# Softmax attention and windowed attention, gated together: other landing times for SyncE's transfers in the planner, and another table of thresholds

## The chip, the cores and the metric

The kernel runs on one core of one Trainium2 chip. The metric is the device time of one execution in microseconds (us). Three executions of the kernel before took 815.80, 822.54 and 823.12 us; their median is 822.54 us. One further execution was profiled; it took 826.73 us, and the span from its first to its last instruction is 824.9 us.

Short names: PE is TensorE (matmuls; PEld its weight loads), DVE is VectorE, ACT is ScalarE, POOL is GpSimd, SP is SyncE, which issues nearly all DMA transfers.

## What is computed

Two attentions over the same x (2048 tokens, 640 features, 32 heads of 20), mixed by a gate. A is full softmax attention, B a causal one over 8 positions that lie 2 apart.

```python
x = A_x
g = _sigmoid((x * gate_w).sum(-1, keepdims=True))
a = _A_ref(x, A_wqkv, A_wo)      # softmax(q k^T / sqrt(20)) v, all 2048 keys, then @ wo
b = _B_ref(x, B_wqkv, B_wo)      # keys at s, s-2, ..., s-14 only, then @ wo
return g * a + (1 - g) * b
```

## The kernel before, in words

**Work on attention A.** The 2048 queries are cut in four chunks of 512, the heads in eight groups of four; that makes 32 groups (`GROUPS`), worked one after the other. A group has 16 key blocks x 4 heads = 64 units. For one unit PE multiplies a 128-key block with 512 queries (L1553) into a PSUM bank, the exponential is taken, and PE multiplies the result with v into the bank `obank` (L1617). The exponential of most units is ACT's (L1576, two or three units in one instruction, called a tile). The four units of a key block may instead go to DVE, as a "quad": DVE turns the scores into int16 numbers that are read as bf16 powers of two (L1566, "ride"), then adds a constant three times (L812), and PE multiplies all four versions with weighted copies of v (`vS`, made by POOL at L805). So a unit on DVE relieves ACT and costs DVE and PE more. At a group's end `gen_norm` (L773) transposes, divides and gates the result, and SP moves it into `oTd` with 4 or 5 transfers (L792).

**The queries.** `gen_qd` (L660) projects 128 features of q at a time: SP loads the weights `WqP` (`wq_load`, L634), PE multiplies, DVE scales into `dst`, SP spreads the rows over the padded `qT` buffers with 3, 7 or 8 transfers (L681), and a bound on the score goes in with 4, 8 or 12 small ones (L721).

**Work on attention B.** Eight units u of 256 tokens. For each, `gen_bproj` projects q, k, v; `gen_b` (L873) multiplies q with shifted k on DVE (L883), sums on PE, takes maximum and exponential, and sends a reciprocal to all partitions by SP in two steps (`rB`, L965 with 4 transfers and L967 with 3). `gen_v4` (L1013) has SP write shifted copies of v into `stage` with 16 transfers (L1017); DVE multiplies them by the probabilities (L981), PE sums, DVE writes `oB` (L1006). `gen_fold` and, at the end, `gen_prefold`, `gen_prefold2` and `tail` multiply `oTd` and `oB` with the output weights.

**The order of the work** is fixed when the kernel is built, by a planner in the kernel's own source. `_Sched.task` (L194) keeps a planned time for each engine: an instruction starts when its engine is free and what it depends on has ended, and ends after a duration that the caller names. For a DMA step the caller names the time from issue to landing; SP is held for `iss * nd`, 0.75 us for each of the `nd` transfers, whatever the landing time:

```python
        if dma:
            self.avail[stream] = start + iss * nd
            t.end = start + dur
```

Side work (everything but scores, exponentials and v products) consists of generators that yield requests such as `("dve", ahead, ready)`; `step` (L1170) grants one only when the planned clock says that its input is ready and its engine is not too far ahead. `ready` and `free` (L167, L175) read the planned ends. So a landing time is a promise on which the order of PE's, DVE's and ACT's instructions is built. On the chip every engine then works off its list in that order and waits on semaphores: if a transfer lands later than promised, the engine whose list has the reader next stands still, with everything behind it in its list.

`PLAN` (L50) sets 21 thresholds anew at tile numbers 0, 10, 20, ... (in the main loop from L1724): how much a tile may be followed by side work (`SLACK`), how late a third bank may come free (`XTOL`), when a quad may be opened for DVE (`DWAIT`, `DIDLE`, `DIDLE2`, `DTIME`, read in `wanted`, L1429), below which PE load filler matmuls are put in (`FILL`, read in `filler`, L1624), and so on. The kernel before has 721 tiles and 90 quads (360 rides at L1566).

Of the kernel before, what the change touches and what calls it, by code (L numbers as in the profile page):

```python
# [334 lines left out]
def _build(ctx, nc, A_x, A_wqkv, A_wo, B_wqkv, B_wo, gate_w, out):  # L335
# [4 lines left out]
    T = sch.task  # L340
# [18 lines left out]
    WqP = sb([P, CN, P], BF16, "WqP")  # L359
# [24 lines left out]
    TQ = TOK // 4  # L384
    tB = sb([P, TQ], FP32, "tB")
    rQ = sb([P, TQ], FP32, "rQ")
# [20 lines left out]
    rB = sb([P, TOK], FP32, "rB")  # L407
# [252 lines left out]
    def gen_qd():  # L660
        while not done.get(("q", 1)):
            yield ("cond",)
        n = 0
# [1148 lines left out]
```

## Time and profile before

| What | Value |
|---|---|
| three executions | 815.80, 822.54, 823.12 us |
| profiled execution | 826.73 us, span 824.9 us |
| ACT busy | 786.5 us (95%), of it L1576 775.1 us in 721 instructions |
| PE busy | 762.3 us (92%) |
| DVE busy | 708.6 us (86%) |
| POOL busy | 146.8 us (18%) |
| mean granted TensorE clock | 0.993 |
| first exponential starts, last one ends | 19.6 us, 812.2 us |

The profile is read from the engine that is busy nearly all the time towards what makes it stand still. "Idle" of an engine is listed with what ended it: `A <- B: total, times, longest`. The planner's own times are not in the profile; the profile has only what the chip did. The trace also has the time at which each transfer's semaphore was raised; a landing time below is the time from the start of the first issue of a step to the last of these.

### The profile page before, as it was taken

How to read it: one execution, taken by the hardware profiler on the slowest of the kernel's cores; microseconds unless marked ns; L12 is line 12 of the kernel's file. 1: busy time of each engine (PE TensorE's matmuls, PEld its weight loads, DVE VectorE, ACT ScalarE, POOL GpSimd, SP SyncE). 2: the span in 40 equal slices, each digit the busy share in tenths (PEclk: the TensorE clock that was granted, in tenths of full speed). 3: DMA queues.
4: the chain of work that ended last, by engine and by line, in shares of the span. 5: the costliest groups of instructions: out<-in, count | busy, mean ns of one | idle time of the engine just before them, and what ended most of it. 6: DMA issues, size and time to landing. Idle time of an engine off the chain costs nothing.

```text
span 824.9 us, 28923 instructions
## 1 busy us (share of the span) xinstructions
PE 762.3 (92%) x12201; PEld 277.6 (34%) x12201; DVE 708.6 (86%) x1255; ACT 786.5 (95%) x753; POOL 146.8 (18%) x203
## 2 busy tenths in 40 slices
PE   8999999999899999999999999899898999888888
PEld 5332223334333333333333334333332343322223
DVE  7578877698899999989988998899799989998963
ACT  4999999999999999999999999999999999999984
POOL 5040032330112111112111201111011111201110
PEclk9999999999999999999999999999999999999999
DMA  9112222001210311013003111300310030102001
GB/s 312 35 27 52 46 46 72 18 14 34 64 36 21 78 23 36 22 23 76 20 20 71 33 31 22 78 18 7 74 23 21 23 78 18 33 21 63 6 6 35
DMA packets 61397, 35.72 MB, mean 43 GB/s; under 512 B 27204, under 2 KB 60068, under 8 KB 61268
## 3 DMA queue, kind: packets, MB, share of 16 engines
q1 hardware_dynamic: 60980, 33.54, 16.5%
q8 instruction: 97, 1.59, 0.8%
q10 hardware_dynamic: 288, 0.33, 0.1%
q14 instruction: 32, 0.26, 0.1%
HBM read 11.94 MB, written 2.62 MB: 18 GB/s over the span
## 4 chain that ended last, share of the span: by engine, by line
ACT 34%; PE 28%; issue 16%; DVE 15%; SPq 4%; DMA 2%; POOL 0%; ACTq 0%; DVEq 0%
ACT ebuf L1576 33%; PE score L1553 8%; PE side L574 7%; PE obank L1617 7%; SPq L1017 4%; DVE uD L812 4%; DVE uD L1566 3%; DVE stage L883 3%; PE score L574 2%; DVE stage L981 1%; DMA stage<-qkvB 1%; DVE qkvB L867 1%; DMA oTd<-oN 1%; PE score L1265 1%; PE obank L475 1%
## 5 line engine op out<-in xcount | busy, mean ns | idle before, releaser
L1576 ACT ACTIVATE ebuf<-score 128x1024 bf16<-128x1024 f32 (+2 forms) x721 | 775.1, 1241 | 17.4 <-PE score L1553 16.7
L1553 PE MATMUL score<-qT,kT 32*128 32x512 bf16 x2048 | 288.0, 386 | 42.2 <-ACT ebuf L1576 28.6
L1566 DVE TENSOR_SCALAR uD<-score 128x512 int16<-128x512 f32 x360 | 240.7, 680 | 27.7 <-PE score L1553 26.2
L812 DVE TENSOR_SCALAR uD<-uD 128x2048 int16<-128x2048 int16 x270 | 185.7, 708 | 15.5 <-PE obank L1617 14.2
L1617 PE MATMUL obank<-ebuf,vA 128*21 128x512 bf16 x1688 | 167.6, 388 | 2.8 <-POOL vS L805 1.2
L1553 PEld LDWEIGHTS score<-qT,kT 32*128 32x128 bf16 x2048 | 70.6, 91 | 285.4 <-ACT ebuf L1576 211.7
L805 POOL TENSOR_TENSOR vS<-vA,vw 128x252 bf16<-128x252 bf16 x90 | 69.4, 777 | 301.4 <-PE obank L1617 277.8
L574 PE MATMUL side<-xT,kvw 128*32 128x256 bf16 (+2 forms) x2320 | 97.9, 286 | 4.2 <-DVE qkvB L867 2.8
L1617 PE MATMUL obank<-uD,vS 128*21 128x512 bf16 x1080 | 96.7, 385 | 0.1
L1617 PEld LDWEIGHTS obank<-ebuf,vA 128*21 128x21 bf16 x1688 | 41.4, 88 | 102.4 <-issue 75.1
L574 PEld LDWEIGHTS side<-xT,kvw 128*32 128x32 bf16 (+1 forms) x2320 | 55.3, 96 | 37.6 <-issue 15.0
L781 POOL TENSOR_TENSOR rcp<-rcp,gA 128x16 f32<-128x16 f32 x31 | 7.6, 247 | 310.9 <-DVE rcp L779 310.9
L981 DVE TENSOR_TENSOR stage<-stage,eB 128x1280 bf16<-128x1280 bf16 x64 | 53.0, 856 | 6.8 <-DMA stage<-qkvB 6.8
L883 DVE TENSOR_TENSOR stage<-qkvB 128x1280 bf16<-128x1280 bf16 x64 | 52.0, 841 | 0.2
L867 DVE CAST qkvB<-side 128x512 bf16<-128x512 f32 (+1 forms) x62 | 36.0, 590 | 3.2 <-PE side L574 3.1
L787 POOL TENSOR_TENSOR oN<-oTt,rcp 128x512 bf16<-128x512 f32 x31 | 32.6, 1052 | 2.4
L574 PE MATMUL side<-woBp,oB 128*32 128x512 bf16 (+1 forms) x540 | 29.1, 317 | 3.6 <-DMA oTd<-oN 1.6
L1617 PE MATMUL obank<-uD,vA 128*21 128x512 bf16 x360 | 32.3, 385 | 0.0
L574 PE MATMUL side<-woA_d,oTd 128*32 128x512 bf16 (+1 forms) x540 | 29.8, 309 | 0.0
L1617 PEld LDWEIGHTS obank<-uD,vS 128*21 128x21 bf16 x1080 | 26.0, 91 | 9.6 <-issue 3.0
L775 DVE STREAM_TRANSPOSE oTt<-obank 128x512 f32<-128x512 f32 x32 | 22.6, 706 | 3.4 <-PE obank L1617 3.3
L1638 PE MATMUL side<-xT,ident 128*32 128x512 bf16 x324 | 24.2, 381 | 0.0
(182 smaller groups left out, 535.7 us busy)
## 6 DMA issues: line engine op xcount, KB each, us to landing
stage<-qkvB SPq DMA_DIRECT2D x128, 82.5 KB
WqP<-in_A_wqkv_dram SPq DMA_DIRECT2D x16, 160.0 KB
stage<-in_B_wqkv_dram SPq DMA_DIRECT2D x1, 2400.0 KB
oTd<-oN SPq DMA_DIRECT2D x108, 20.0 KB
qT<-dst SPq DMA_DIRECT2D x104, 20.0 KB
out_dram<-outsb SPq DMA_DIRECT2D x12, 160.0 KB
kvw<-in_A_wqkv_dram SPq DMA_DIRECT2D x2, 800.0 KB
oTd<-in_A_x_dram SPq DMA_DIRECT2D x2, 640.0 KB
```

What stands on the lines that cost most here:

```text
L574: ins = e.matmul(o[j:k, :], l(j) if callable(l) else l[:, j:k], r, start=(first and i == 0), stop=(last and i == n - 1), skip_group_check= ...
L787: T(en, c2, lambda e: e.tensor_tensor(oo, ii, ib, ALU.mult), reads=["rcp", "oTt"], writes=["oN0"])
L805: T("pool", 0.7, lambda e: e.tensor_tensor(vS[:, d % NVS, :, :], _ap(vA, (kb * NQ + q) * 4 * DV, [[0, K - 1], [1, 4 * DV]]), _ap(vw, 0, [[ ...
L812: T("dve", 0.066 + 0.1334 * n, lambda e, k=k: e.tensor_scalar(uD[u][:, 0:512 * n].bitcast(I16), uD[u][:, 0:512 * n].bitcast(I16), SHIFTS[k ...
L867: t = TB(dvc(n * TOK), lambda e, o=o, i=i: e.tensor_copy(o, i), reads=[("side", b)], writes=[key])
L883: TB(dvc(CN * TOK, 2), lambda e, w=w, ks=ks: e.tensor_tensor(prodB(w), qB[:, :, :], ks, ALU.mult), reads=["qB", "kB"], writes=[("prod", w) ...
L981: TB(dvc(CN * TOK, 2), lambda e, o=o, vs=vs, ee=ee: e.tensor_tensor(o, vs, ee, ALU.mult), reads=["eB", ("prod", k)], writes=[("prod", k + ...
L1017: T("sp", 12.0, lambda e: [e.dma_start(bass.AP(tensor=stage, offset=32 * w4 * 4 * CN * (VW + TOK) + c * VW, ap=[[4 * CN * (VW + TOK), 32], ...
L1553: ins = e.matmul(o, kT[32 * j:32 * j + 32, q, kb * P:(kb + 1) * P], qT[g % NQT][32 * j:32 * j + 32, :], start=True, stop=True)
L1566: t = T("dve", 0.6, lambda e: e.tensor_scalar(uD[d % NU][:, 512 * i:512 * (i + 1)].bitcast(I16), side[x], UOFF, 0.0, op0=ALU.add, op1=ALU. ...
L1576: exps[s] = T("act", actc(512 * n), lambda e: e.activation(ebuf[s % NE][:, 0:512 * n], score[s % 2][:, 0:512 * n], ACTF.Exp, scale=LN2 / S ...
L1617: ins = e.matmul(obank[32 * j:32 * j + DV, :], v, src, start=(kb == 0), stop=(last and k >= len(lst) - 4), skip_group_check=True)
```

## The change

Seven charges, all of DMA steps on SP, get other landing times; `iss`, the number of transfers and all dependencies stay. And all rows of `PLAN` are replaced (64 before, 67 after); the code that reads it is the same.

| step | transfers | charge before (us) | charge after (us) |
|---|---|---|---|
| L637 weights to `WqP` | 1, 2 | 3.0, 3.5 | 4.5, 5.0 |
| L681 rows to `qT` | 3, 7, 8 | 3.5, 5.5, 6.0 | 4.24, 7.36, 8.14 |
| L721 bounds to `qT` | 4, 8, 12 | 4.0, 6.0, 8.0 | 4.5, 7.1, 9.7 |
| L792 results to `oTd` | 4, 5 | 4.0, 4.5 | 5.02, 5.8 |
| L965 reciprocals | 4 | 4.0 | 4.7 |
| L967 reciprocals | 3 | 3.5 | 4.2 |
| L1017 shifted v | 16 | 12.0 | 13.8 |

```diff
-        T("sp", 2.5 + 0.5 * len(parts), lambda e: [e.dma_start(WqP[:, :, a:a + n], wA_v[:, :, d:d + n]) for a, d, n in parts],
+        T("sp", 4.0 + 0.5 * len(parts), lambda e: [e.dma_start(WqP[:, :, a:a + n], wA_v[:, :, d:d + n]) for a, d, n in parts],
...
-                T("sp", 2.0 + 0.5 * len(pc), lambda e, i=i, pc=pc, qc=qc: [e.dma_start(
+                T("sp", 1.9 + 0.78 * len(pc), lambda e, i=i, pc=pc, qc=qc: [e.dma_start(
...
-                T("sp", 2.0 + 0.5 * 4 * len(runs), lambda e, runs=runs, qc=qc: [e.dma_start(
+                T("sp", 1.9 + 0.65 * 4 * len(runs), lambda e, runs=runs, qc=qc: [e.dma_start(
...
-            T("sp", 2.0 + 0.5 * len(pc), lambda e: [e.dma_start(
+            T("sp", 1.9 + 0.78 * len(pc), lambda e: [e.dma_start(
...
-        T("sp", 2.0 + 0.5 * 4, lambda e: [e.dma_start(rB[0:32, j * TQ:(j + 1) * TQ], rQ[32 * j:32 * j + 32, :]) for j in range(4)],
+        T("sp", 4.7, lambda e: [e.dma_start(rB[0:32, j * TQ:(j + 1) * TQ], rQ[32 * j:32 * j + 32, :]) for j in range(4)],
...
-        spread = lambda: T("sp", 2.0 + 0.5 * 3, lambda e: [e.dma_start(rB[32 * i:32 * i + 32, :], rB[0:32, :]) for i in range(1, 4)],
+        spread = lambda: T("sp", 4.2, lambda e: [e.dma_start(rB[32 * i:32 * i + 32, :], rB[0:32, :]) for i in range(1, 4)],
...
-        T("sp", 12.0, lambda e: [e.dma_start(
+        T("sp", 13.8, lambda e: [e.dma_start(
```

The rows of `PLAN` have the columns SLACK (two numbers), XTOL, XPRIO, XLATE, DWAIT, DIDLE, DIDLE2, DTIME, DLOW, DLATE, DVE_AHEAD, DAHEAD, BOOST, XBOOST, RFILL, FILL, HOLD, BOFF, BNEED, PVMIN, MAXQ. Three of the rows, before and after:

```diff
-    0: ((0.3, 0.64), 0.32, 2.5, 2.5, 0.49, -1.3, -0.1, 11.8, 7.0, 7.2, 0.52, 0.47, 4.4, 4.0, 0.0, 0.75, 2, -3, 0.38, 4.0, 3.0),
+    0: ((0.3, 0.64), 0.37, 2.5, 2.5, 0.49, -1.3, -0.1, 11.87, 7.0, 7.2, 0.52, 0.47, 4.4, 4.0, 0.0, 0.75, 2, 0.0, 0.45, 4.0, 4.0),
...
-    450: ((0.35, 0.67), 0.21, 6.6, 2.5, 0.78, -1.31, 0.45, 12.98, 6.7, 7.79, 0.67, 0.71, 4.6, 5.77, 0.08, 0.69, 2, 0, 0.55, 4.0, 3.0),
+    450: ((0.32, 0.67), 0.69, 2.5, 2.5, 0.8, -1.3, 0.24, 12.65, 6.7, 8.73, 0.57, 0.52, 4.4, 4.5, 0.01, 0.67, 1, -3, 0.45, 4.0, 2.0),
...
-    650: ((0.35, 0.67), 0.21, 2.5, 2.5, 0.78, -1.31, 0.45, 12.98, 4.5, 7.79, 0.77, 0.71, 5.28, 5.56, 0.08, 0.69, 1, 0, 0.46, 4.0, 3.0),
+    650: ((0.36, 0.66), 0.6, 2.5, 6.6, 0.49, -1.52, -0.25, 12.98, 7.0, 6.67, 0.52, 0.53, 4.4, 4.0, -0.04, 0.78, 2, 1, 0.49, 4.0, 3.0),
```

Over the 721 tiles, each row weighted by the tiles for which it holds, the mean of `DIDLE2` goes from 0.14 to -0.03, of `DIDLE` from -1.35 to -1.47, of `XTOL` from 0.30 to 0.56, of `FILL` from 0.69 to 0.77.

125 rows, old and new, of the table PLAN are left out of this document.

## The prediction

> **What bounds the kernel now.** I read the busy times first, then what ended ACT's idle time, then the timelines around its largest gaps, then the granted clock there.
>
> ```profile
> PE 762.3 (92%) x12201; PEld 277.6 (34%) x12201; DVE 708.6 (86%) x1255; ACT 786.5 (95%) x753; POOL 146.8 (18%) x203
> ```
>
> ACT is the bound: its exponentials run from 19.6 to 812.2 us, and only 17.4 us in between are idle. Time comes from there: from ACT's idle time, or from units that go to DVE. The waits of ACT, DVE and PE (us in total, times, longest) say who ends idle time:
>
> ```profile
> ACT ebuf L1576 <- PE score L1553: 16.7, 16, 2.4
> DVE stage L981 <- DMA stage<-qkvB: 6.8, 4, 2.1
> PE side L574 <- DMA oTd<-oN: 1.6, 1, 1.6
> ```
>
> ACT waits for scores alone, so the question is what made the scores late. The second and third line are candidates: DVE stood four times for the shifted copies of v, PE once for a group's result. Two timelines show one of them from both sides. DVE, then ACT:
>
> ```profile
> 529.67 0.69 DVE L812 TENSOR_SCALAR uD<-uD 128x2048 int16<-128x2048 int16 x1
> 532.46 0.82 DVE L981 TENSOR_TENSOR stage<-stage,eB 128x1280 bf16<-128x1280 bf16 x1 [2.10 <-DMA stage<-qkvB]
> ```
>
> ```profile
> 531.82 2.81 ACT L1576 ACTIVATE ebuf<-score 128x1536 bf16<-128x1536 f32 x2
> 536.31 1.02 ACT L1576 ACTIVATE ebuf<-score 128x1024 bf16<-128x1024 f32 x1 [1.68 <-PE score L1553]
> 538.24 1.02 ACT L1576 ACTIVATE ebuf<-score 128x1024 bf16<-128x1024 f32 x1 [0.91 <-PE score L1553]
> 539.75 2.37 ACT L1576 ACTIVATE ebuf<-score 128x1536 bf16<-128x1536 f32 x2 [0.48 <-PE score L1553]
> ```
>
> DVE's list has L981 next and stands for 2.10 us; the evictions of qkvB behind it come late, PE waits 2.12 us for one (a projection is next in its list, then scores), and 1.4 us after DVE went on ACT runs dry, three times in a row. The same picture stands at three other places. ACT near the end of the span:
>
> ```profile
> 794.87 4.13 ACT L1576 ACTIVATE ebuf<-score 128x1536 bf16<-128x1536 f32 x3
> 801.40 1.45 ACT L1576 ACTIVATE ebuf<-score 128x1536 bf16<-128x1536 f32 x1 [2.39 <-PE score L1553]
> 803.46 1.45 ACT L1576 ACTIVATE ebuf<-score 128x1536 bf16<-128x1536 f32 x1 [0.61 <-PE score L1553]
> ```
>
> and PE there, with the fold ahead of the scores in its list:
>
> ```profile
> 798.94 1.87 PE L574 MATMUL side<-woBp,oB 128*32 128x512 bf16 x16 [1.63 <-DMA oTd<-oN]
> 800.74 0.61 PE L1553 MATMUL score<-qT,kT 32*128 32x512 bf16 x3
> ```
>
> The busy times by stretch (PE, PEld, DVE, ACT, POOL, then the granted clock) show what follows such a stop:
>
> ```profile
> 532.80:536.20 3.40, 1.54 (x46) 1.09 (x46) 3.40 (x7) 1.83 (x2) 0.59 (x1) 1.00 0.03 9
> 536.20:539.60 3.40, 3.40 (x32) 0.70 (x29) 2.83 (x6) 2.05 (x2) 1.11 (x1) 0.50 0.00 0
> ```
>
> After a stretch in which PE was busy for 1.54 of 3.40 us, the clock is 0.50 for the next 3.4 us; this is why ACT runs dry again at 538 and 540. The clock's records have just three such windows between the start and the tail, at 536.2, 597.6 and 799.0 us, each behind a landing wait.
>
> **ACT's idle time by cause.** Behind the wait at 216.5 us: 1.42. Behind 532.5: 1.68 + 0.91 + 0.48 = 3.07. Behind 594.3: 1.98 + 0.69 + 0.91 = 3.58. Behind 798.9: 2.39 + 0.61 = 3.00. Sum 11.07 of 17.4 us. The rest is 2.05 at 21 us, before any of these steps, and bits of at most 0.5.
>
> **The change part by part.** It removes and adds no instruction of its own; it moves them. Its charges against the landing times in the trace (shortest, median, longest):
>
> - L1017, 12.0 to 13.8: traced 12.6, 13.6, 15.2. The longest three (14.2, 14.7, 15.2) are those behind which ACT ran dry; a fourth wait of 0.9 us cost ACT nothing.
> - L792, 4.5 to 5.8 for five transfers: traced 4.7, 5.0, 6.7; the 6.7 is the one before the fold.
> - L681 with seven, 5.5 to 7.36: traced 6.4, 6.8, 7.9. L721 with twelve, 8.0 to 9.7: traced 8.4, 9.0, 9.4; with eight, 6.0 to 7.1: traced 5.3, 5.4, 6.1.
> - L965, 4.0 to 4.7: traced 3.6, 4.2, 5.0. L967, 3.5 to 4.2: traced 3.0, 3.1, 4.3. L637, 3.0 to 4.5: traced 2.4, 2.5, 4.5.
>
> So the old charges were short of the trace where an engine stood (L1017, L792, L681), and the new ones are above the median everywhere, for L637 by 2.0 us.
>
> *Term 1, the waits for shifted v.* They were 1.83, 2.10, 1.98 and 0.9 us. With readers placed 1.8 us later, 0.03, 0.30, 0.18 and 0 are left. *Term 2, the fold.* PE stood 2.1 us from the end of its matmuls (their records leave 1.63); L792 gets 1.3 more, so 0.8 is left. Together 1.3 us of waits remain, and I charge ACT with the same 1.3. The clock windows should go with the waits: 11.07 - 1.3 = 9.8 us saved. Bounds: nothing, if landings slip as much again; all 11.1, if none does. What is late next at these places is the scores behind L981's neighbours, which are ACT's normal feed.
>
> *Term 3, what the larger charges push back.* The q chain (L637, L681, L721) is planned up to 1.5 + 1.86 + 1.1 = 4.5 us later for each group. It is hidden: q of a group landed 25 us or more before the group ahead of it closed, in all groups from the fourth on, and 12.7 us in the one before. In group 2 it was 4.6 us (landed at 72.2, group 1 closed at 76.8); scores start some 2.7 us (three tiles) before a close, so with that cover gone 4.5 - (4.6 - 2.7) = 2.6 us once. I take 0, since scores waited for qT only 0.2 us in the whole span. The B chain gets 1.8 + 0.7 + 0.7 = 3.2 us for each of 8 units, 25.6 if none of it is hidden; the last L1006 starts at 769.6 and the fold at 798.9, so 29 us hide it. If it were not hidden, POOL's copies and SP's later steps behind L1017 would be late too; I take 0. SP's own list is charged 0.75 us for a transfer as before, and is idle 129 us before L637 alone.
>
> *Term 4, the table.* No row shows where it leads, since it changes every decision. Its currency is the quad. An exponential of two units takes 0.90 us from start to start, one of three 1.33, so a unit is 0.44 to 0.45 us and a quad 1.8 us of ACT; on DVE it is four rides and three shifts at about 0.6 us from start to start, 4.2 us. Gain at most: DVE is idle 56 us between 170 and 790 us, 13 quads, 23 us, though that idle time is in bits of 1 us. Loss at most: from 100 us on, stretches of 50 us held 4.0 to 7.7 quads with a mean of about 6; the leanest throughout would be 2 fewer in each of 14, 28 quads, 50 us. The columns lean to the gain: DIDLE2 falls from a mean of 0.14 to -0.03, so quads open while DVE is less idle, and FILL rises, which keeps PE busier. But a threshold is no count; I take 0, nearest to the row that stays, 90 quads.
>
> **Sum.** 826.7 - 9.8 = 816.9 on the profiled execution. The median of the three shown, 822.54, is 4.2 us lower than it. If the unprofiled executions have all of these stops, the time is 822.5 - 9.8 = 812.7; if the profiled one merely had more of them (the fastest, 815.8, is 10.9 below it, about the size of the 11.07), it is 816.9. I take the middle, 815.
>
> A rule to weigh: the Trainium skill ("TensorE: Matmul & The Clock Gate", Part 1) has the clock halve after at least one idle window of about 3.4 us. PE's stops here were 2.1 to 2.2 us and the clock fell all the same, so the trace does not bear out a whole idle window as the condition.
>
> **Rivals.**
>
> 1. *The low clock is not the stops' doing*, and three such windows stay wherever they fall. For it: one stop (216.5 us, PE waits as DVE stood 1.83) had no window behind it. Against: all three windows stand behind stops. Then only ACT's first gaps go, 1.42 + 1.68 + 1.98 + 2.39 = 7.5, less 1.3: 6.2 us saved, 815 + 3.6 = 818.6. The skill's rule, taken by its word, would lead here.
> 2. *The waits move.* Landings of L1017 spread over 2.6 us, and a new order puts other transfers beside them (14.2 to 15.2 where L792, L965 or L967 followed closely). If they slip again by what they slipped, nothing is gained: 822.
> 3. *The table gives DVE more*: four quads more, 815 - 7.2 = 808. For it DIDLE2 and DVE's 6.8 us of waits that come free (1.6 quads); against it PE at 92%.
> 4. *Slower: the table gives DVE less*, because the planner now sees DVE's inputs and banks come later and refuses quads in `wanted`. Price 1.8 us for each quad. It undoes the 7.5 us gained against the median at four quads lost, and is slower by 1% (above 830.8) from nine lost, so 81 or fewer; 833 at ten. For it: the leanest stretches above. Against: DIDLE2.
>
> **How the numbers follow.** Chances: likeliest (815, give or take 5) 0.45; rival 1 0.10; rival 2 0.12; rival 3 0.15; rival 4 0.18. A difference of 1% is about what a measurement of this kernel can tell from none: 814.3 to 830.8 counts as the same. A little under half of the likeliest lies below 814.3 (0.22), with rival 3 that makes 0.37 faster; the other 0.23 with rivals 1 and 2 makes 0.45 the same; 0.18 slower. Range: 805, which leaves out rival 3 with six or more quads (0.05), to 830, which leaves out most of rival 4 (0.14).
>
> **What the profile of the changed kernel would show.** Terms 1 and 2: DVE's wait at L981 for stage under 1.5 us in total, PE's for oTd under 1, ACT's idle time before L1576 about 8 us in place of 17.4, no or one window of clock 0.50 between 20 and 810 us. Term 3: scores waiting for qT still under 1 us, and the last L1006 before 797. Term 4: rides at L1566, now 360; each four are 1.8 us. Wrong it would be if the count of rides is under 324, or if ACT is idle as long as before behind other waits.

## The result, and the profile after

The kernel after takes 814.56 us (median of 11 executions, 813.62 to 815.09), the kernel before 820.05 us in the same comparison (11 executions, 815.80 to 823.59): ratio 0.9941, 95% interval 0.9918 to 0.9965, so 5.5 us or 0.6% less. The profiled executions differ by more: 826.73 us before, 815.09 us after, spans 824.9 and 813.3 us. The executions of the kernel after also lie within 1.5 us, those of before within 7.8 us.

The busy times of the kernel after, and its waits (us in total, times, longest):

```profile
PE 772.4 (95%) x12439; PEld 279.5 (34%) x12441; DVE 704.3 (87%) x1248; ACT 787.4 (97%) x758; POOL 138.9 (17%) x202
```

```profile
ACT ebuf L1579 <- PE score L1556: 5.7, 7, 2.1
```

ACT's waits for scores fall from 16.7 to 5.7 us, and 4.1 of these are the two at the start that were there before (2.09 us ahead of the first exponential, 2.05 us ahead of the one at 23 us). (Line numbers are three higher in the kernel after: L984 was L981, L1020 was L1017.) No line of DVE's waits names a landing of `stage` any more and none of PE's a landing of `oTd`. DVE where the largest landing stood nearest to its reader, then PE at the last fold:

```profile
219.01 0.69 DVE L815 TENSOR_SCALAR uD<-uD 128x2048 int16<-128x2048 int16 x1
219.79 1.56 DVE L984 TENSOR_TENSOR stage<-stage,eB 128x1280 bf16<-128x1280 bf16 x2
221.27 0.68 DVE L1569 TENSOR_SCALAR uD<-score 128x512 int16<-128x512 f32 x1
```

```profile
788.47 0.61 PE L1620 MATMUL obank<-uD,vS 128*21 128x512 bf16 x8
788.90 0.61 PE L577 MATMUL side<-woBp,oB 128*32 128x512 bf16 x8
789.44 0.39 PE L1556 MATMUL score<-qT,kT 32*128 32x512 bf16 x3
```

At 219.79 L984 begins 0.02 us after its landing, with DVE busy until 219.70: the new order has no slack at this place. At 788.9 the fold begins 6.2 us after SP issued L795 (782.69), with scores right behind it instead of a stop of 1.63 us (by the matmul records). The clock's records have no window at half speed between the start and the tail.

Where the 11.6 us between the two spans are (before, then after: busy, mean ns, idle before):

```profile
L1576 ACT ACTIVATE ebuf<-score 128x1024 bf16<-128x1024 f32 (+2 forms) x721 | 775.1, 1241 | 17.4 <-PE score L1553 16.7
L1579 ACT ACTIVATE ebuf<-score 128x1024 bf16<-128x1024 f32 (+1 forms) x726 | 776.0, 1235 | 6.6 <-PE score L1556 5.7
```

ACT's idle time before its exponentials went from 17.4 to 6.6 (10.8 less); the end after the last exponential from 12.7 to 11.1 (1.6 less); the exponentials themselves from 775.1 to 776.0 busy (0.9 more), as there are 356 rides instead of 360. The remaining 0.1 is rounding and the start.

### The profile page after: what moved, and what is told of

It reads as the page before. It is cut to its first block, busy times and chain, and to the rows that moved or that the text cites. A ratio compares the mean times of both kernels' runs of the same rounds, so it can differ in the third digit from the quotient of the medians.

```text
span 813.3 us, 29378 instructions
## 1 busy us (share of the span) xinstructions
PE 772.4 (95%) x12439; PEld 279.5 (34%) x12441; DVE 704.3 (87%) x1248; ACT 787.4 (97%) x758; POOL 138.9 (17%) x202
## 4 chain that ended last, share of the span: by engine, by line
ACT 41%; PE 29%; issue 17%; DVE 12%; SPq 1%; DMA 0%; ACTq 0%; DVEq 0%
ACT ebuf L1579 40%; PE score L1556 9%; PE obank L1620 7%; PE side L577 5%; DVE uD L815 3%; DVE uD L1569 3%; PE score L577 2%; DVE stage L984 1%; SPq L1020 1%; DVE stage L886 1%; DVE qkvB L870 1%; PE side L1641 1%; PE score L1268 1%; PE obank L478 1%; PE obank L1641 1%
## 5 line engine op out<-in xcount | busy, mean ns | idle before, releaser
L1579 ACT ACTIVATE ebuf<-score 128x1024 bf16<-128x1024 f32 (+1 forms) x726 | 776.0, 1235 | 6.6 <-PE score L1556 5.7
L1569 DVE TENSOR_SCALAR uD<-score 128x512 int16<-128x512 f32 x356 | 238.3, 681 | 29.7 <-PE score L1556 28.2
L808 POOL TENSOR_TENSOR vS<-vA,vw 128x252 bf16<-128x252 bf16 x89 | 62.3, 710 | 280.0 <-PE obank L1620 247.0
L577 PE MATMUL side<-xT,kvw 128*32 128x256 bf16 (+1 forms) x2300 | 95.7, 283 | 1.6 <-DVE qkvB L870 1.0
L577 PEld LDWEIGHTS side<-xT,kvw 128*32 128x32 bf16 x2300 | 55.2, 96 | 32.8 <-issue 14.6
L984 DVE TENSOR_TENSOR stage<-stage,eB 128x1280 bf16<-128x1280 bf16 x64 | 52.2, 843 | 0.1
L1641 PE MATMUL side<-xT,ident 128*32 128x512 bf16 x404 | 30.0, 382 | 0.0
L577 PE MATMUL side<-woA_d,oTd 128*32 128x128 bf16 (+3 forms) x540 | 29.0, 298 | 0.0
L1641 PE MATMUL obank<-xT,zero 128*32 128x512 bf16 x328 | 26.8, 381 | 0.0
```

The lines of the kernel that those rows point to most:

```text
L577: ins = e.matmul(o[j:k, :], l(j) if callable(l) else l[:, j:k], r, start=(first and i == 0), stop=(last and i == n - 1), skip_group_check= ...
L808: T("pool", 0.7, lambda e: e.tensor_tensor(vS[:, d % NVS, :, :], _ap(vA, (kb * NQ + q) * 4 * DV, [[0, K - 1], [1, 4 * DV]]), _ap(vw, 0, [[ ...
L984: TB(dvc(CN * TOK, 2), lambda e, o=o, vs=vs, ee=ee: e.tensor_tensor(o, vs, ee, ALU.mult), reads=["eB", ("prod", k)], writes=[("prod", k + ...
L1569: t = T("dve", 0.6, lambda e: e.tensor_scalar(uD[d % NU][:, 512 * i:512 * (i + 1)].bitcast(I16), side[x], UOFF, 0.0, op0=ALU.add, op1=ALU. ...
L1579: exps[s] = T("act", actc(512 * n), lambda e: e.activation(ebuf[s % NE][:, 0:512 * n], score[s % 2][:, 0:512 * n], ACTF.Exp, scale=LN2 / S ...
L1641: ins = e.matmul(o[32 * j:32 * j + 32, :], w[:, 32 * j:32 * j + 32] if best else w[:, :], xT[:, 0, 0:512], start=bool(best), stop=bool(bes ...
```

## The experiments

Two theories. W: the new charges place readers where the transfer has landed, so that no engine stops, and that is the gain. T: the new table makes a better order by itself (more fillers, wider tiles). The first four runs, and the two with one and with six transfers more, keep an order of PE, DVE, ACT and POOL exactly as it is and move only the landing on the chip; this is done with fewer or more transfers in one step of SP, whose charge for issuing is kept in sum. So they change the wait and nothing that is planned. On the chip SP's later steps move a little with it, since SP issues its transfers one after the other (16 of them at L1017 took 11.0 to 12.7 us in the kernel before). The times below come from three comparisons in which the kernel before took 820.05, 819.11 and 819.28 us, so a difference of up to 0.9 us between two comparisons tells nothing.

### The order of before, shifted v landing earlier

```diff
-  ... for w4 in range(4) for c in range(4)],
-  reads=["vB"], writes=[("prod", w) for w in range(WIN)], dma=True, nd=16)
+  ... for w4 in range(4) for c in range(4) if w4 < 3 or c < 1],
+  reads=["vB"], writes=[("prod", w) for w in range(WIN)], dma=True, nd=13, iss=12.0 / 13)
```

> The kernel before with the instructions of PE, DVE, ACT and POOL in the same order, one for one; of the 16 transfers at L1017 three are left out (three shifted copies of v are missing from the output), SP's charge for issuing stays 12.0 us in all. So L1017 lands some 3 x 0.72 = 2.2 us earlier on the chip while the order knows nothing of it. Theory W (the gain came from landings that no longer stop an engine): the waits of 1.83, 2.10, 1.98 and 0.9 us at L981 go to under 0.3 in total, ACT's idle time falls by the 8.07 us behind them, from 17.4 to about 9.3, of the three windows of half clock only the one at 799 us stays, and a profiled span of about 817. Against the median of before, 820.05, which the profiled execution exceeds, 3 to 8 us: ratio 0.990 to 0.996. Rival T (the gain came from the other order that the table makes, its fillers and its wider tiles; the waits were a side matter that ACT would have lost anyhow): the order is the same, so less than 1 us, ratio 0.999 or above.

Measured: 814.51 us, ratio 0.9945 (0.9918 to 0.9972), span 812.8 us. L1017 landed 10.8 to 12.9 us after its first issue instead of 12.6 to 15.2. The waits of ACT and the landing waits that are left:

```profile
ACT ebuf L1576 <- PE score L1553: 6.1, 7, 2.1
DVE stage L981 <- DMA stage<-qkvB: 0.5, 1, 0.5
PE side L574 <- DMA oTd<-oN: 1.1, 1, 1.1
```

ACT lost as little as in the kernel after, with not one instruction of ACT, DVE or PE moved. That is against T, and it shows that the old order was as good as the new one but for its late landings. One part of the expectation missed: L792 landed 6.2 us after its first issue in place of 6.7, the stop before the fold was 1.08 us in place of 1.63, it cost ACT 0.80 in place of 3.00, and no window of half clock followed. So the span is 812.8 us, not about 817.

### The same, and the last result but one landing earlier

```diff
-  pc = [... if h // 4 == q]
-  T("sp", 2.0 + 0.5 * len(pc), ... dma=True, nd=len(pc))
+  pc = [... if h // 4 == q]; npc, pc = len(pc), pc[:3 if g == NG - 2 else 5]
+  T("sp", 2.0 + 0.5 * npc, ... dma=True, nd=len(pc), iss=0.75 * npc / len(pc))
```

> As the first, and of the five transfers at L792 for the last group but one two are left out as well (their rows of oTd keep older values, so a part of the last chunk's output is wrong), with SP's charge unchanged; the other engines' order is again that of before. L792 lands some 2 x 0.72 = 1.4 us earlier ahead of the fold at 799 us. Theory W: of PE's 2.1 us stop 0.7 is left, ACT's 3.0 us behind it shrink to about 1, no window of half clock is left before the tail, ACT idle 7 us in all, profiled span 813 to 815, time 814 to 816, ratio 0.991 to 0.995 and a spread between executions as small as that of the kernel after (1.5 us) in place of 7.8. Rival T: ratio 0.999 or above, spread as before.

Measured: 813.93 us, ratio 0.9937 (0.9913 to 0.9961), span 811.4 us. PE does not wait for `oTd` any more (0.7 us was expected), ACT waits 5.2 us for scores, no half clock. Against the first run that is 0.6 us, too little to tell. The span came out below the 813 to 815 us expected, and the spread did not fall to 1.5 us: 813.17 to 817.12.

### The order of after, shifted v landing later

```diff
-  ... for w4 in range(4) for c in range(4)],
-  reads=["vB"], writes=[("prod", w) for w in range(WIN)], dma=True, nd=16)
+  ... for w4 in range(4) for c in range(4)] + [e.dma_start(spare[32 * c:32 * c + 32, :], vB[32 * c:32 * c + 32, 0, 0:VW]) for c in range(3)],
+  reads=["vB"], writes=[("prod", w) for w in range(WIN)] + ["spare"], dma=True, nd=19, iss=12.0 / 19)
```

> The kernel after with the other engines' order unchanged; L1020 gets three more transfers (528 bytes on each of 32 partitions, into a spare buffer), SP's charge for issuing stays 12.0 us. So it lands some 1.8 to 2.2 us later than the order was made for; everything is computed. In the kernel after, the first L984 follows the landing by 0.02, 6.9, 0.6, 0.6, 5.5, 5.3, 20 and 1.2 us, so four of eight would wait: 2.1, 1.5, 1.5 and 0.9 us. Theory W: those waits appear at L984, ACT's idle time grows from 6.6 us by 4 to 8 with one or two windows of half clock, time 818 to 822, ratio 0.998 to 1.003, and executions differ by several us again. Rival T: DVE waits but ACT has scores in store, so time stays within 1 us of 814.6, ratio 0.993 to 0.995.

Measured: 822.04 us, ratio 1.0029 (1.0003 to 1.0055): 7.5 us over the kernel after, and the whole gain is gone. Its waits, and ACT around one of them:

```profile
ACT ebuf L1579 <- PE score L1556: 12.2, 12, 3.3
DVE stage L984 <- DMA spare<-qkvB: 5.4, 3, 2.8
```

```profile
378.74 5.54 ACT L1579 ACTIVATE ebuf<-score 128x1536 bf16<-128x1536 f32 x4
387.55 2.79 ACT L1579 ACTIVATE ebuf<-score 128x1536 bf16<-128x1536 f32 x2 [3.27 <-PE score L1556]
```

DVE stood 2.79 us for the landing at 382.24; ACT ran dry 2 us later, for 3.27 us. T expected less than 1 us in all. Three places waited (2.11, 2.79 and 0.49 us) where four were expected.

### The order of after, shifted v landing earlier

The edit is that of the first run, made to the kernel after.

> The kernel after with the other engines' order unchanged and three of the 16 transfers at L1020 left out (three shifted copies of v are missing from the output): it lands 2.2 us earlier than the order was made for. Theory W: nothing waits for it any more, so nothing is gained: 814.2 to 814.8, ratio 0.993 to 0.995. Rival T: the same. A third account, that the transfers themselves slow other work (DMA traffic beside other engines' reads and writes), would show here and in the first run as time that falls without a wait: 0.3 us or more below 814.5.

Measured: 813.96 us, ratio 0.9924 (0.9899 to 0.9949). ACT waits 5.7 us for scores, as in the kernel after. That is 0.5 us below 814.5 and so fits the third account, which asked for 0.3 or more; but the kernel before was 0.9 us lower in this comparison too, so it cannot be told from nothing. In the new order the shifted v is not late any more, and a cost of its traffic is not shown. The second and this run compare like with like, 13 transfers in the old order and in the new: 813.93 and 813.96 us.

### One or six transfers more

The edit is that of the third run, with one transfer more (`nd=17`) and with six (`nd=22`, of 256 bytes for each partition).

> The kernel after with the other engines' order unchanged; L1020 gets one more transfer (into a spare buffer), so it lands some 0.65 us late; everything is computed. First readers follow the landing by 0.02, 6.9, 0.6, 0.6, 5.5, 5.3, 20 and 1.2 us in the kernel after: waits of about 0.6, 0.1 and 0.1 us. If late landings cost what they last (1 us for 1 us): 0.5 to 0.8 us, 815.1 to 815.4. If a stop under about 1 us is covered by the scores that ACT has in store, and only a longer one takes the clock down for 3.4 us: 814.4 to 814.8, no change.

> The same with six more transfers, so L1020 lands some 3.7 us late: waits of about 3.7, 3.1, 3.1 and 2.5 us at four of the eight places, 12.4 in all, none at the four with 5 us or more. If late landings cost what they last, less about 0.9 us each that ACT has in store: 814.5 + 8.8, 822 to 825. If each also takes the clock down for 3.4 us, which cost ACT some 1.4 us more behind each stop in the kernel before: 814.5 + 14, 827 to 832. With three more transfers it was 822.0, 7.5 us over.

Measured: 816.07 us with one (ratio 0.9967, 0.9944 to 0.9991), 829.93 us with six (1.0127, 1.0092 to 1.0162). The waits with one:

```profile
ACT ebuf L1579 <- PE score L1556: 6.7, 10, 2.1
DVE stage L984 <- DMA spare<-qkvB: 0.7, 1, 0.7
DVE qbnd L711 <- DMA qT<-qbnd: 0.5, 1, 0.5
```

and with six:

```profile
ACT ebuf L1579 <- PE score L1556: 19.4, 17, 4.8
DVE stage L984 <- DMA spare<-qkvB: 13.4, 4, 4.3
```

| transfers at L1020 | waits at L984 | ACT waits for scores | windows of half clock | time | over the kernel after |
|---|---|---|---|---|---|
| 16 | 0 | 5.7 | 0 | 814.56 | |
| 17 | 0.7 | 6.7 | 0 | 816.07 | 1.5 |
| 19 | 5.4 | 12.2 | 2 | 822.04 | 7.5 |
| 22 | 13.4 | 19.4 | 3 (one twice as long) | 829.93 | 15.4 |

With one, the time lies above both accounts. The profile gives a part of it: behind the 0.73 us wait at 220.7 ACT falls 0.6 us behind the kernel after, so little of it was covered; behind the 0.47 us wait of L711 at 322.8 it loses nothing; and it loses 0.6 us at 518 us, where PE stood 0.71 us for nothing that the profile shows. That the one transfer made L711's landing (L724) late is not shown, since with three more transfers L711 did not wait. With six, the higher account held. With three and with six a wait of 1 us costs 1.4 and 1.1 us; for waits under 1 us the runs show no one price (0.9 us cost nothing in the kernel before, 0.7 us cost 0.6 here).

### Charges without the table, table without the charges

> The kernel after with the table PLAN of before: the new charges alone. Every decision of the planner falls otherwise, so the order is a third one; it has 344 rides (before 360, after 356) in 712 tiles. Theory W: the landing waits at L981 and before the fold go as in the kernel after, whatever the table; 16 units more for ACT cost 16 x 0.45 = 7 us, so 820 to 825 if the table's thresholds are good for any order. What speaks against that: they hold from fixed tile numbers on, so with the order shifted they meet other work, and side work that is then forced ahead of scores leaves ACT idle for long; then tens of us more, 850 to 950, with DVE's waits for landings still small. Rival T (the new table is what gained): no better than before in either case.

> The kernel before with the table PLAN of after: the new table with the old charges. 360 rides in 716 tiles, more filler matmuls than either kernel. Rival T: the table's looser XTOL and higher FILL do the work, 813 to 817. Theory W: the readers are again placed by charges that are 1 to 2 us short, so waits of 1 to 3 us at L981 come back, 3 us of ACT's idle time for each that is over 1.5 us, 820 to 830; and if thresholds fit only the order that they were set for, tens of us more, 850 to 920, of which the landing waits are the smaller part.

Measured, two executions each: 947.44 us (ratio 1.156, 1.149 to 1.163) with the new charges and the old table; 924.17 us (1.128, 1.121 to 1.135) with the old charges and the new table. ACT's waits, charges only and then table only:

```profile
ACT ebuf L1576 <- PE score L1553: 111.9, 19, 31.5
ACT eB L930 <- PE score L926: 11.3, 1, 11.3
```

```profile
ACT ebuf L1579 <- PE score L1556: 62.2, 23, 24.2
ACT eB L933 <- PE side L929: 42.7, 1, 42.7
```

PE in the first of them, where ACT ran dry for 31.5 us (some rows left out):

```profile
129.94 0.39 PE L1553 MATMUL score<-qT,kT 32*128 32x512 bf16 x3
...
137.38 2.33 PE L574 MATMUL side<-xT,WqP 128*32 128x512 bf16 x20 [5.51 <-DMA WqP<-in_A_wqkv_dram]
...
150.63 2.88 PE L574 MATMUL score<-kvw,xT 128*32 128x320 bf16 x40
...
162.80 0.61 PE L1553 MATMUL score<-qT,kT 32*128 32x512 bf16 x6
```

For 32 us PE has no scores in its list. It waits for the weights of a projection of q, makes it, and works off a pile of v projections; by the code that is what `run_until(("q", gn))` in the main loop does when a group's q is not planned yet: it forces whatever side work there is. That the call is the cause is read from the order of the work; no run took it out. So neither half was of use alone. The table's thresholds hold from fixed tile numbers on, and with other charges the work at those tiles is other work. The two runs bear out the second half of both expectations, with misses: 924.17 us lies above the 920 that was expected at most; landing waits were expected to be small in the one and 1 to 3 us each in the other, and DVE waited 13.4 us at L981, 6.9 us for bounds and 4.8 us for `oTd` in the first, 14.0 us at L984 (11.9 of them once) in the second. What the table is worth by itself cannot be read from them. What the new order is worth beyond its landings can be read from the first two runs, which keep the old order and take away its late landings: 814.51 and 813.93 against 814.56 us, nothing. No run changes one charge alone; of the seven, only L1017 and L792 were tried, by their landings.

## Why the prediction was right

**The likeliest case.** 815 us was forecast, 814.56 measured, and by the mechanism named: the stops at L981 and at the fold went, the clock windows with them, and the time of the other engines' work hardly moved.

**Terms 1 and 2, 9.8 us of ACT's idle time.** The profiles differ by 10.8 us there. The term was too small by 1.0 us, since the 1.3 us of waits that it left standing are gone: the landings of L1020 in the new order reached 14.0 us at most, where those of L1017 before reached 15.2. The fold is not reached in PE's list until 6.2 us after the issue of L795, which landed after 4.9 us, where L792 before the fold had taken 6.7. That the landings themselves came shorter was not foreseen. Two readings were off without harm to the sum: the 17.4 us of idle time also hold 2.09 us ahead of the first exponential, and PE's stop of 2.1 us before the fold is 1.63 us in the records, so 0.3 us would have been left of it, not 0.8.

**The step from the profiled execution to the median** was the weak one. The saving was worked out on an execution with more stops than most, and 820.05 - 814.56 = 5.5 us is what the median gives; the forecast had 822.54 - 815 = 7.5. That the middle between "all have these stops" and "only this one" came out right to half a microsecond is luck: the base was 2.5 us too high and the saving 2.0 us too large. The executions show what lies behind the step. Of 34 of the kernel before, ten with a mean granted clock of 1.000 took 814.8 to 817.8 us, twelve with 0.996 or less 820.1 to 824.6: with the same order and the same charges, some executions have windows of half clock (each takes 0.002 from the mean) and some have not. Two small sums that the forecast lacked nearly cancel: the end became 1.6 us shorter, which no step had, and the exponentials 0.9 us longer.

**Term 3, nothing for the larger charges.** Right: scores waited 0.2 us for qT as before, and the last L1009 starts at 749.8 us, earlier than the 769.6 of L1006.

**Term 4, nothing for the table.** Nearly: 89 quads for 90. DIDLE2's lean to more quads did not come about. In the second run, with the old order and hardly a late landing (0.4 us at L981), the exponentials take 780.0 us from the first to the last, in the kernel after 782.7. Of these 2.6 us 2.0 are the exponentials' own time (774.0 busy, after 776.0), close to the price of the one quad, and 0.7 idle time.

**Rival 1, the low clock not the stops' doing.** Ruled out by the runs with one order and different landings. The old order had three such windows with late landings and none without; the new order has none, and two and three with late landings. All eight stand behind stops, and none of these runs has one elsewhere before the tail. The one thing that spoke for the rival was a stop at 216.5 us without a window; PE's part in it was the shortest of the four, 1.45 us (below).

**Rivals 2 to 4** (waits move, more quads, fewer quads) did not come about. Rival 4's price, 1.8 us for a quad, could not be tested beyond one quad.

## What to carry to other kernels

Where an order is fixed ahead, ask of each landing how late it may be: the slack between landing and first reader, place by place, is the number, and landings that came 2 to 4 us late cost more than the waits lasted here, 1.1 to 1.4 us for 1 us, since the engine behind the wait feeds the one that bounds the kernel. To learn what an order loses to a late transfer, keep the order and move the landing; changing the planner's input gives another kernel. And a median is not the profiled execution: count in the profile what only some executions have before taking a saving from it.

## What the runs showed of the hardware

The granted clock goes by stretches of a fixed grid. The windows of half clock in the kernel before start at 536.19, 597.63 and 799.02 us; their distances are 18.0 and 59.0 times 3.413 us. Laid on this grid, the stretch just before each window is the one to look at (stretch, its length, then PE, PEld, DVE, ACT and POOL busy, then the clock), in the kernel before:

```profile
215.34:218.75 3.41, 1.96 (x41) 0.87 (x37) 2.22 (x4) 1.99 (x3) 1.47 (x2) 1.00 0.17 35
532.78:536.19 3.41, 1.53 (x43) 1.08 (x43) 3.41 (x7) 1.85 (x2) 0.61 (x1) 1.00 0.04 9
594.22:597.63 3.41, 1.75 (x24) 0.66 (x28) 3.34 (x6) 1.43 (x3) 0.00 (x0) 1.00 0.07 15
795.61:799.02 3.41, 1.78 (x26) 0.40 (x27) 2.50 (x4) 3.39 (x3) 0.00 (x0) 1.00 0.07 17
```

and with six transfers more in the order of after:

```profile
382.56:385.97 3.41, 1.88 (x26) 0.43 (x22) 0.03 (x1) 3.41 (x3) 0.00 (x1) 1.00 0.06 10
```

In the runs with these two orders, eight stretches at full clock had PE busy for 1.88 us or less of 3.41 by the matmul records, and the next stretch ran at half clock eight times of eight; with 1.96 us (the stop at 216.5) and more it did not. A stretch that was itself at half clock, with 0.83 us, was followed by another, so that this window lasted 6.8 us:

```profile
385.97:389.38 3.41, 0.83 (x18) 0.62 (x22) 3.41 (x7) 0.49 (x1) 0.91 (x1) 0.50 0.01 2
389.38:392.80 3.42, 3.42 (x42) 1.23 (x38) 2.53 (x4) 1.56 (x2) 0.00 (x0) 0.50 0.32 108
```

The edge is not sharp by these records, of which some can be missing. With the old charges and the new table one stretch with 1.84 us was followed by full clock (1.00 up to 572.97 us):

```profile
402.31:405.73 3.42, 1.84 (x43) 0.98 (x43) 3.42 (x6) 2.67 (x2) 0.66 (x1) 1.00 0.01 2
```

So PE need not stand for a whole stretch; some 45% of one was enough here. The rule weighed in the prediction (the Trainium skill, "TensorE: Matmul & The Clock Gate", Part 1) asks for a whole idle window, and these traces do not agree with that. Where a stop falls on the grid matters too. With the new charges and the old table PE stood 2.00 us, from 159.03 to 161.03, over the edge between two stretches, and the clock stayed full:

```profile
156.97:160.39 3.42, 2.06 (x64) 1.30 (x52) 2.77 (x5) 0.00 (x0) 1.27 (x1) 1.00 0.00 0
160.39:163.80 3.41, 1.95 (x30) 0.56 (x30) 2.12 (x4) 0.56 (x1) 1.19 (x3) 1.00 0.00 0
163.80:167.21 3.41, 3.07 (x40) 0.72 (x32) 2.97 (x7) 3.41 (x5) 3.29 (x4) 1.00 0.04 11
```

The 1.63 us before the fold fell into one stretch, and the next ran at half clock. The Trainium skill's page also says, in the same part, that the window is 3413 ns and free-running, which the distances above bear out. The stop before the fold had both prices: it was 1.63 us with a window behind it (3.00 us of ACT) in the kernel before, and 1.08 us without one (0.80 us) in the first run; how much of the difference is the window's and how much the shorter stop's is not shown.
